# A gated mix of long convolution and attention on one core: five probability tiles instead of four, one copy instead of two of two small tiles

## The chip, the core and the metric

The kernel runs on one core of a Trainium2 chip. The time is device microseconds (us) of one execution; the number that counts is the median of several executions. The engines are TensorE (PE in the profile, its weight loads PEld), VectorE (DVE), ScalarE (ACT), GpSimd (POOL) and SyncE (SP), whose queue issues most of the DMAs.

## What is computed

For x of 2048 tokens by 640, the result is `g * a + (1 - g) * b`, with a gate g per token. Cut to what matters:

```python
g = sigmoid((x * gate_w).sum(-1, keepdims=True))
# a: a shifted product kv = (4-tap shift of k) * v, convolved with a 2048-tap filter per channel
kv = k_shift * v
y = irfft(rfft(kv, 4096) * rfft(ssm_k, 4096))[:2048] + kv * ssm_D
a = q * y                                  # q is x
# b: attention of 32 heads of width 20 over one shared k and v
scores = einsum("bhqd,bkd->bhqk", x @ wq, x @ wk) * 20 ** -0.5
b = einsum("bhqk,bkd->bhqd", softmax(scores), x @ wv) @ wo
out = g * a + (1 - g) * b
```

## The kernel before, in words

The attention is cut into 512 rounds (u = 0 to 511): four blocks of 512 queries (index I), eight groups of four heads (g) in each, sixteen chunks of 128 keys (j) in each group. A round has, for four heads, 128 keys and 512 queries:

- QK (L897 to L912): four matmuls of 21 rows each that work side by side in the array and write four PSUM banks, that is two pairs of banks. There are three such pairs (banks 0 to 5), used in turn.
- EXP (L914 to L922): two instructions of ScalarE, h = 0 and h = 1, each over one pair of banks (128x1024), which write bf16 probabilities to one of the tiles ET0 to ET3. The slot is `(2 * u + h) % 4`. In rounds j = 2 and j = 9 of most groups VectorE computes h = 1 instead, in five instructions (DEXP, L924 to L940), into the tile ETd.
- PV (L948 to L968): four matmuls of 32 columns each, side by side, that add probabilities times v into bank 6. After sixteen rounds VectorE copies bank 6 out (`acc`, L1002), and a chain of small DMAs and VectorE instructions divides by the sum and stores the group (`norm`, L998 to L1015).

The program's order of the attention on PE is fixed: after EXP(u, 0) come QK(u+1), EXP(u, 1) and PV(u-1) (L976 to L993). The rest of the kernel, the convolution as cosine and sine matmuls (L1098 to L1214, spectra, product on GpSimd, inverse), query projections (`qproj`, L832) and the output projection (`oproj`, L1217), is put between these by a list scheduler (L133 to L370). It runs a clock of its own with assumed costs and places, on each engine, what is ready: on PE the next attention matmul if it is ready, else a group of other matmuls that fits in the gap (L237 to L303). Where its own account of PE is under half busy in the last 2.4 us and a gap is left, it places a matmul over a tile of zeros that is there only to keep PE working (L290 to L294, emitted from L1278). The order that comes out is then static; at run time each engine works through its list in order and waits on semaphores, one for each dependence on another engine's instruction, a tile's earlier reader among them.

Two small tiles belong to the change as well. `cr` (two copies, L602) holds a row that VectorE writes (L862) and a DMA takes into the query tile (L865). `ytmp` (two copies, L617) holds the sum that VectorE makes of an inverse group (L1208) and that the next VectorE instruction multiplies (L1212).

The output projection has eight groups of five matmuls per block I. The groups of blocks 0 to 2 may use bank 7 alone (L1230), so that each waits for VectorE's copy of the one before (L1235).

Of the kernel before, what the change touches and what calls it, by code (L numbers as in the profile page):

```python
# [479 lines left out]
class Kernel:  # L480

    def __init__(self, nc, aps):
        self.nc = nc
        self.aps = aps
        self.g = Graph()
        self.T = {}
        self.nb = 0
        self.late_pv = []


# [47 lines left out]
    def alloc(self):  # L538
# [30 lines left out]
        sb("Tsin0", [128, NF, 128], BF16)  # L569
        sb("Tsinv0", [128, 1024], BF16)  # L570
        sb("zeros", [128, 128], BF16)
        for i in range(4):
            sb(f"ET{i}", [128, 1024], BF16)
        sb("ETd", [128, 1024], BF16)
        sb("dJ", [128, 1024], dt.uint32)
# [23 lines left out]
        for i in range(4):  # L599
            sb(f"sq{i}", [128, 512], BF16)  # L600
        sb("ci", [16, 512], I32)
        for i in range(2):  # L602
            sb(f"cr{i}", [16, 512], BF16)
        sb("acc", [128, 512], F32)
        sb("den", [128, 16], F32)
        sb("rcp", [128, 16], F32)
# [7 lines left out]
                 ("vslab0", [128, D], BF16), ("vslab1", [128, D], BF16), ("vslab2", [128, D], BF16),  # L614
                 ("kprod", [128, 4, D], BF16), ("kshs", [128, 2, D], BF16), ("w4", [128, 4, D], BF16)]
        late = [("AB0", [128, NF, 2, 2, CW], BF16), ("AB1", [128, NF, 2, 2, CW], BF16),
                ("ytmp0", [128, 512], BF16), ("ytmp1", [128, 512], BF16)]  # L617
        spec = []
        for i in range(3):
            spec += [(f"X{i}", [128, 2, 2, CW], BF16), (f"K{i}", [128, 2, 3, CW], BF16)]  # L620
# [211 lines left out]
    def qproj(self, I, gs, prio, banks, ng):  # L832

        T = self.T
        qt = T[f"qT{I % 2}"]
        par = I % 2
        for gl, gi in enumerate(gs):
            gr = self.group("qp", prio, banks=banks)
            for dc in range(NDC):
                self.mm(gr, lambda e, bk, gi=gi, dc=dc: e.matmul(  # L840
                    self.bank(bk), T["wq_pad"][:, dc, 128 * gi:128 * gi + 128],
                    T["xT"][:, dc, 512 * I:512 * I + 512], start=(dc == 0), stop=(dc == NDC - 1)),
                    [("wq_pad", 0 if gi < 2 else 1), ("xT", I)], c_mm(512))
            self.evac(gr, "dve", None, (), [("qT", par, gi)], 0.7,
                      alts=self.copy_alts(qt[:, gi, :], lambda bk: self.bank(bk)))
            self.dve(lambda e, gi=gi, gl=gl: e.tensor_tensor(T[f"sq{gl}"][:, :], qt[:, gi, :], qt[:, gi, :],
                                                             ALU.mult),
                     [("qT", par, gi)], [("sq", gl)], c_fast(512), prio=prio - 500, port=True, name="sq")
        gr = self.group("q2", prio - 500, banks=banks)
        ind = T[f"IndG{ng}"]  # L850
        for gl in range(ng):
            self.mm(gr, lambda e, bk, gl=gl: e.matmul(self.bank(bk)[0:4 * ng, :], ind[:, gl, :], T[f"sq{gl}"][:, :],
                                                      start=(gl == 0), stop=(gl == ng - 1)),
                    [f"IndG{ng}", ("sq", gl)], c_mm(512))
        n = 4 * ng
        self.nb += 1
        ck = self.nb % 2
        ci, cr = T["ci"], T[f"cr{ck}"]
        self.evac(gr, "dve", lambda e, bk: e.tensor_scalar(
            ci[0:n, :], self.bank(bk)[0:n, :].bitcast(I32), 0.5, float(0x1FBD1DF5), ALU.mult, ALU.add), (),  # L860
            ["ci"], c_ps(512))
        self.dve(lambda e: e.tensor_scalar(cr[0:n, :], ci[0:n, :].bitcast(F32), T["kmaxr"][0:n, 0:1], -UP,  # L862
                                           ALU.mult, ALU.add), ["ci", "kmaxr"], [("cr", ck)], c_fast(512), prio=prio - 500,
                 name="root")
        o = self.dma(qt[20:128:32, gs[0]:gs[0] + ng, :], cr[0:n, :], reads=[("cr", ck)],  # L865
                 writes=[("qT", par, gi) for gi in gs], nbytes=n * 1024, prio=prio - 500, name="crow")
        if I == 0 and gs[0] == 0:
            self.crow0 = [o]
# [20 lines left out]
    def attention(self, I):  # L889
# [23 lines left out]

        def EXP(u, h):  # L914
            p = pairs(u)[h]
            slot = (2 * u + h) % 4
            if h == 1 and on_dve(u):
                return DEXP(u, p)
            op("act", lambda e, p=p, slot=slot: e.activation(  # L919
                T[f"ET{slot}"][:, :], self.ps[:, 1024 * p:1024 * p + 1024], ACT.Exp, scale=SCALE),  # L920
                [("ps", 2 * p), ("ps", 2 * p + 1)], [("ET", slot)], 0.91, name="exp", main=True,
                after=self.sins if u == 0 else ())  # L922
# [25 lines left out]
        def PV(u):  # L948
            j = u % 16
            rs = (0, 1) if on_dve(u) else (0, 1, 2, 3)  # L950
            for r in rs:
                slot = (2 * u + r // 2) % 4
                o = PVmm(r, j, T[f"ET{slot}"], ("ET", slot), cost=0.03 if r < rs[-1] else 0.27, main=True,
                         cont=(r > 0), banks=(6,))
                o.last = j == NSC - 1
# [225 lines left out]
    def inverse(self, c, q, prio):  # L1181
        T = self.T
        AB = T[f"AB{c % 2}"]
        n = 4 * c + q
        yt = T[f"ytmp{n % 2}"]
        gr = self.group("inv", prio)
        for h in range(2):
            ci = 2 * q + h
# [12 lines left out]
        def toks(t):  # L1201
# [5 lines left out]
        rk = [("kvc", c, 0), ("kvc", c, 1), ("kvc", c, 2), ("kvc", c, 3)]  # L1207
        self.evac(gr, "dve", lambda e, bk: e.tensor_tensor(  # L1208
            y4, self.bank(bk).rearrange("p (i b c) -> p i b c", i=2, b=2), kvp, ALU.add), rk,
            [("ytmp", n % 2)], c_ps(512))  # L1210
        ids = [2 * q, 2 * q + 1, NF + 2 * q, NF + 2 * q + 1]
        self.dve(lambda e: e.tensor_tensor(kvp, y4, xg, ALU.mult),  # L1212
                 [("ytmp", n % 2)] + [("xg", i) for i in ids], [("A", i) for i in ids],
                 c_fast(512), prio=prio - 1000, port=True, name="amul", after=())  # L1214


# [116 lines left out]
```

## Time and profile before

| what | value |
| --- | --- |
| runs | 1022.82, 1033.32, 1030.26 us; median 1030.26 |
| the profiled execution | 1036.53 us, span 1034.7 us |
| mean TensorE clock in it | 0.95 |
| first EXP starts, last EXP starts | 43.4, 984.9 us |
| busy in the span: PE, DVE, ACT, POOL | 837.3, 641.0, 936.3, 384.0 us |

The span runs from the first to the last instruction; the time holds 1.8 us more. All durations come from this one execution, which lies 6.3 us above the median of the three runs. The busy time of ScalarE is a union of its instructions, and consecutive ones overlap a little, so that a short wait of one can hide as less overlap; a gap is named as a wait only from 150 ns up.

### The profile page before, as it was taken

The page shows a single profiled execution, that of the slowest core. Times are in us where ns is not written, and L with a number is a line of the kernel's source. Part 1 is how long each engine was busy: PE and PEld are TensorE (multiplying, and loading weights), DVE is VectorE, ACT ScalarE, POOL GpSimd, SP SyncE. Part 2 cuts the span into 40 slices and gives each one's busy share as a digit, 9 for nine tenths or more (in the row PEclk, how much of TensorE's full clock was granted, in tenths as well). Part 3 has the DMA queues.
Part 4 walks back from the last instruction along what each step waited for, and adds up shares of the span by engine and source line. Part 5 has one row for each costly group of instructions (what it writes and reads, how often), then busy time and mean ns, then how long its engine had stood idle before and what let it go on. Part 6 is the DMA issues. An engine that isn't in the chain of part 4 may idle for free.

```text
span 1034.7 us, 16679 instructions
## 1 busy us (share of the span) xinstructions
PE 837.3 (81%) x6874; PEld 348.6 (34%) x6949; DVE 641.0 (62%) x954; ACT 936.3 (90%) x1007; POOL 384.0 (37%) x427
## 2 busy tenths in 40 slices
PE   6677777888888888888888888887888988888865
PEld 4122113433334333344333333442234433323322
DVE  8577972336675677655676666665775566644632
ACT  6499999998899999999999999998999999998910
POOL 2360000784154336651316541434652546620000
PEclk9799999998899999999999999998899999998985
DMA  5312731001000000000000100000000000012221
GB/s 149 122 33 91 237 104 54 11 12 37 16 17 17 12 18 27 17 16 17 16 18 16 37 18 12 15 9 16 16 17 17 17 16 12 12 54 57 67 76 42
DMA packets 34626, 40.57 MB, mean 39 GB/s; under 512 B 12796, under 2 KB 27766, under 8 KB 34550
## 3 DMA queue, kind: packets, MB, share of 16 engines
q1 hardware_dynamic: 32582, 39.25, 12.1%
q8 instruction: 54, 0.88, 0.4%
q10 hardware_dynamic: 1968, 0.26, 0.2%
q14 instruction: 22, 0.18, 0.1%
HBM read 32.03 MB, written 7.08 MB: 38 GB/s over the span
## 4 chain that ended last, share of the span: by engine, by line
ACT 69%; PE 22%; DMA 5%; DVE 3%; issue 1%; SPq 0%; ACTq 0%
ACT ET L919 68%; PE ps L903 5%; PE ps L943 5%; PE ps L1122 4%; PE ps L1197 3%; PE ps L1232 2%; DMA rbc<-scr_d 2%; PE ps L840 1%; DVE outsb L1235 1%; PE ps L1278 1%; DMA qT<-cr 1%; DMA scr_d<-rcp 1%; PE ps L784 0%; DMA xn<-in_A_q_dram 0%; DMA wo<-in_B_wo_dram 0%
## 5 line engine op out<-in xcount | busy, mean ns | idle before, releaser
L919 ACT ACTIVATE ET<-ps 128x1024 bf16<-128x1024 f32 x972 | 912.7, 1021 | 35.9 <-PE ps L943 26.5
L1160 POOL TENSOR_TENSOR Pp<-X,K 128x256 f32<-128x256 bf16 x240 | 198.7, 854 | 404.6 <-DVE K L1150 272.4
L903 PE MATMUL ps<-qT,kT 21*128 21x512 bf16 x2048 | 227.7, 395 | 146.5 <-ACT ET L919 137.9
L943 PE MATMUL ps<-ET,vaug 128*32 128x512 bf16 x1944 | 210.8, 398 | 0.4 <-ACT ET L919 0.4
L903 PEld LDWEIGHTS ps<-qT,kT 21*128 21x128 bf16 x2048 | 56.6, 91 | 316.8 <-ACT ET L919 304.9
L1160 POOL TENSOR_TENSOR V<-Pp 128x256 f32<-128x256 f32 x80 | 70.7, 884 | 69.9 <-DVE AB L1177 67.1
L943 PEld LDWEIGHTS ps<-ET,vaug 128*32 128x32 bf16 x1944 | 52.6, 93 | 118.9 <-issue 115.3
L931 DVE TENSOR_SCALAR dJ<-ps 128x1024 uint32<-128x1024 f32 x52 | 63.6, 1224 | 45.9 <-PE ps L903 45.5
L1278 PE MATMUL ps<-Tcos,zeros 128*128 128x512 bf16 x252 | 80.6, 401 | 6.2 <-issue 6.2
L1197 PE MATMUL ps<-AB,Tcos 128*128 128x256 bf16 x320 | 77.3, 278 | 2.3 <-DVE ytmp L1208 2.0
L938 DVE SCALAR_TENSOR_TENSOR dJ<-dJ 128x1024 f32<-128x1024 uint16 x52 | 70.4, 1353 | 0.4
L936 DVE SCALAR_TENSOR_TENSOR dE<-dJ,dE 128x1024 f32<-128x1024 uint16 x52 | 69.0, 1328 | 0.5
L939 DVE SCALAR_TENSOR_TENSOR ETd<-dJ,dE 128x1024 bf16<-128x1024 f32 x52 | 69.2, 1330 | 0.2
L1197 PE MATMUL ps<-AB,Tsin 128*128 128x256 bf16 x280 | 68.5, 278 | 0.0
L1160 POOL TENSOR_TENSOR Pp<-Pp 128x512 f32<-128x512 f32 x40 | 59.9, 1498 | 2.8
L1002 DVE COPY acc<-ps 128x512 f32<-128x512 f32 x32 | 22.1, 691 | 61.7 <-PE ps L943 61.6
L1139 DVE TENSOR_SCALAR K<-ps 128x256 bf16<-128x256 f32 x35 | 14.8, 423 | 58.8 <-PE ps L1122 58.7
L1012 DVE TENSOR_TENSOR oTn<-acc,rbc 128x512 bf16<-128x512 f32 x32 | 27.6, 862 | 37.3 <-DMA rbc<-scr_d 37.2
L1232 PE MATMUL ps<-wo,oTp 128*128 128x320 bf16 x160 | 36.5, 370 | 17.2 <-DVE outsb L1235 13.7
L1122 PE MATMUL ps<-kv,Tsin 128*128 128x256 bf16 x320 | 49.8, 279 | 0.0
L1122 PE MATMUL ps<-ssm_kT,Tsin 128*128 128x256 bf16 x320 | 49.7, 281 | 0.0
L1122 PE MATMUL ps<-ssm_kT,Tcos 128*128 128x256 bf16 x320 | 47.7, 282 | 2.3 <-DVE X L1134 1.2
(127 smaller groups left out, 847.4 us busy)
## 6 DMA issues: line engine op xcount, KB each, us to landing
kslab<-in_A_k_dram SPq DMA_DIRECT2D x15, 640.0 KB
rbc<-scr_d SPq DMA_DIRECT2D x32, 256.0 KB
scr_o<-oTn SPq DMA_DIRECT2D x32, 128.0 KB
xn<-in_A_q_dram SPq DMA_DIRECT2D x4, 640.0 KB
vslab<-in_A_v_dram SPq DMA_DIRECT2D x16, 160.0 KB, 4.2
kst<-in_A_ssm_k_dram SPq DMA_DIRECT2D x5, 512.0 KB
oTp<-scr_o SPq DMA_DIRECT2D x16, 160.0 KB, 2.9
out_dram<-outsb SPq DMA_DIRECT2D x16, 160.0 KB
```

The costliest lines, as they stand in the source:

```text
L903: o = op("pe", lambda e, r=r, Iu=Iu, g=g, j=j, bk=banks[r]: e.matmul(self.bank(bk), T["kT4"][32 * r:32 * r + 21, 128 * j:128 * j + 128], T ...
L919: op("act", lambda e, p=p, slot=slot: e.activation(T[f"ET{slot}"][:, :], self.ps[:, 1024 * p:1024 * p + 1024], ACT.Exp, scale=SCALE), [("p ...
L931: V(lambda e, p=p: e.tensor_scalar(J[:, :], self.ps[:, 1024 * p:1024 * p + 1024], SCALE * LOG2E * 65536.0, EOFF * 65536.0, ALU.mult, ALU.add),
L936: V(lambda e: e.scalar_tensor_tensor(Ef, lo, ED, Ef, ALU.add, ALU.mult), ["dJ", "dE"], ["dE"], c_ps(1024), **k)
L938: V(lambda e: e.scalar_tensor_tensor(Jf, lo, EP, lo, ALU.add, ALU.mult), ["dJ"], ["dJ"], c_ps(1024), **k)
L939: V(lambda e: e.scalar_tensor_tensor(T["ETd"][:, :], Jf, EQ, Ef, ALU.add, ALU.mult), ["dJ", "dE"], ["ETd"], c_ps(1024), **k)
L943: return op("pe", lambda e, r=r, j=j, src=src: e.matmul(self.bank(6)[32 * r:32 * r + 32, :], T["vaug"][:, j, :], src[:, 512 * (r % 2):512 ...
L1122: o = self.mm(gr, lambda e, bk, lhs=lhs, rhs=rhs, comp=comp, n=n: e.matmul(self.bank(bk, 256, 256 * comp), lhs, rhs, start=(n == 0), stop= ...
L1160: self.pool(lambda e: e.tensor_tensor(out, a, b, alu), reads, writes, c_pool(n), prio=prio, port=True, name="mac")
L1197: self.mm(gr, lambda e, bk, lhs=lhs, fc=fc, comp=comp, h=h: e.matmul(self.bank(bk, 256, 256 * h), lhs, AB[:, fc, :, comp, :], start=(fc == ...
L1232: self.mm(gr, lambda e, bk, kc=kc, ci=ci, n0=n0: e.matmul(self.bank(bk, HD), op[:, kc, 128 * ci:128 * ci + 128], T["wo"][:, kc, n0:n0 + HD ...
L1278: sch.filler = lambda e: e.matmul(self.bank(6), self.T["zeros"][:, :], self.T["Tcos"][:, 0, 0:512], start=False, stop=False)
```

## The change

A fifth probability tile is added, and the slot of a round's half becomes `(2 * u + h) % 5`. `cr` and `ytmp` have one copy each instead of two.

```diff
-        self.nb = 0
@@ alloc
-        for i in range(4):
+        for i in range(5):
             sb(f"ET{i}", [128, 1024], BF16)
...
-        for i in range(2):
-            sb(f"cr{i}", [16, 512], BF16)
+        sb("cr", [16, 512], BF16)
...
-                ("ytmp0", [128, 512], BF16), ("ytmp1", [128, 512], BF16)]
+                ("ytmp", [128, 512], BF16)]
@@ qproj
-        ci, cr = T["ci"], T[f"cr{ck}"]
+        ci, cr = T["ci"], T["cr"]
...
-                                           ALU.mult, ALU.add), ["ci", "kmaxr"], [("cr", ck)], c_fast(512), prio=prio - 500,
+                                           ALU.mult, ALU.add), ["ci", "kmaxr"], ["cr"], c_fast(512), prio=prio - 500,
...
-        o = self.dma(qt[20:128:32, gs[0]:gs[0] + ng, :], cr[0:n, :], reads=[("cr", ck)],
+        o = self.dma(qt[20:128:32, gs[0]:gs[0] + ng, :], cr[0:n, :], reads=["cr"],
@@ EXP
-            slot = (2 * u + h) % 4
+            slot = (2 * u + h) % 5
@@ PV
-                slot = (2 * u + r // 2) % 4
+                slot = (2 * u + r // 2) % 5
@@ inverse
-        yt = T[f"ytmp{n % 2}"]
+        yt = T["ytmp"]
...
-            [("ytmp", n % 2)], c_ps(512))
+            ["ytmp"], c_ps(512))
...
-                 [("ytmp", n % 2)] + [("xg", i) for i in ids], [("A", i) for i in ids],
+                 ["ytmp"] + [("xg", i) for i in ids], [("A", i) for i in ids],
```

Since the scheduler sees other dependences, its whole order comes out anew: the same matmuls, but 298 instead of 319 over the tile of zeros. Two places on PE follow. Lines of the changed program are 4 or 5 lower (L899 is L903 of before, L939 is L943, L1118 is L1122, L1192 is L1197, L1227 is L1232, L1273 is L1278).

Rounds 204 to 206 on PE, before (qT: QK; ET: PV; zeros: the matmuls over zeros):

```order
L903 MATMUL ps<-qT1,kT4 128x512 x4
L943 MATMUL ps<-ET0,vaug 32x512 x2
L943 MATMUL ps<-ET1,vaug 32x512 x2
L1278 MATMUL ps<-Tcos,zeros 128x512 x2
L903 MATMUL ps<-qT1,kT4 128x512 x4
L943 MATMUL ps<-ET2,vaug 32x512 x2
L943 MATMUL ps<-ET3,vaug 32x512 x2
L1278 MATMUL ps<-Tcos,zeros 128x512 x2
```

The same rounds now:

```order
L899 MATMUL ps<-qT1,kT4 128x512 x4
L939 MATMUL ps<-ET4,vaug 32x512 x2
L939 MATMUL ps<-ET0,vaug 32x512 x2
L1273 MATMUL ps<-Tcos,zeros 128x512 x3
L899 MATMUL ps<-qT1,kT4 128x512 x4
L939 MATMUL ps<-ET1,vaug 32x512 x2
L939 MATMUL ps<-ET2,vaug 32x512 x2
L1118 MATMUL ps<-ssm_kT1_78,Tcos 128x256 x8
```

QK still stands ahead of the PV of two rounds earlier; the tiles go round in fives; a convolution group stands where two matmuls over zeros stood, one round earlier than before.

The end of PE's list, before, from the last QK on (oTp: the output projection):

```order
L903 MATMUL ps<-qT1,kT4 128x512 x4
L943 MATMUL ps<-ET2,vaug 32x512 x2
L943 MATMUL ps<-ET3,vaug 32x512 x2
L943 MATMUL ps<-ET0,vaug 32x512 x2
L943 MATMUL ps<-ET1,vaug 32x512 x2
L1232 MATMUL ps<-wo_84,oTp1_86 128x320 x5
L943 MATMUL ps<-ET2,vaug 32x512 x2
L943 MATMUL ps<-ET3,vaug 32x512 x2
L1232 MATMUL ps<-wo_84,oTp1_86 128x320 x30
L1232 MATMUL ps<-wo_84,oTp0_85 128x320 x40
L1232 MATMUL ps<-wo_84,oTp1_86 128x320 x40
```

And now, right behind the last PV (AB: the inverse of the convolution):

```order
L1192 MATMUL ps<-AB0_80,Tsin 128x256
L1192 MATMUL ps<-AB0_80,Tcos 128x256
L1192 MATMUL ps<-AB0_80,Tsin 128x256
L1192 MATMUL ps<-AB0_80,Tcos 128x256
L1192 MATMUL ps<-AB0_80,Tsin 128x256
L1192 MATMUL ps<-AB0_80,Tcos 128x256
L1192 MATMUL ps<-AB0_80,Tsin 128x256
L1192 MATMUL ps<-AB0_80,Tcos 128x256
L1192 MATMUL ps<-AB0_80,Tsin 128x256
L1227 MATMUL ps<-wo_83,oTp1_85 128x320 x40
L1227 MATMUL ps<-wo_83,oTp0_84 128x320 x40
L1227 MATMUL ps<-wo_83,oTp1_85 128x320 x40
```

Nine matmuls of an inverse group and 24 groups of the output projection now stand behind the last PV, where 22 groups stood behind it before.

The end of SP's queue, before, from the last group's store on (oTp1: loads of the last block's projection input, one for each quarter; outsb: stores of output rows, which wait for the projection):

```order
L501 DMA scr_o<-oTn 128x512
L501 DMA out_0_dram<-outsb0_87 128x640
L501 DMA oTp1_86<-scr_o 32x5x512
L501 DMA out_0_dram<-outsb1_88 128x640
L501 DMA oTp1_86<-scr_o 32x5x512
L501 DMA out_0_dram<-outsb2_89 128x640
L501 DMA oTp1_86<-scr_o 32x5x512
L501 DMA out_0_dram<-outsb3_90 128x640
L501 DMA oTp1_86<-scr_o 32x5x512
```

And now:

```order
L500 DMA scr_o<-oTn 128x512
L500 DMA out_0_dram<-outsb2_88 128x640
L500 DMA oTp1_85<-scr_o 32x5x512
L500 DMA out_0_dram<-outsb3_89 128x640
L500 DMA oTp1_85<-scr_o 32x5x512
L500 DMA out_0_dram<-outsb0_86 128x640
L500 DMA oTp1_85<-scr_o 32x5x512
L500 DMA out_0_dram<-outsb1_87 128x640
L500 DMA oTp1_85<-scr_o 32x5x512
```

The last load stood behind all four stores of block 2 (outsb0 to outsb3); now it stands behind the first two of them.

3 lines of the change are left out of this document (removed).

## The prediction

> **What bounds the kernel now.** I read the page first, then the waits of ScalarE, its exponentials (line L919) by stretches, the timeline of one full-clock round, the clock by stretches, and last the tail.
>
> ```profile
> PE 837.3 (81%) x6874; PEld 348.6 (34%) x6949; DVE 641.0 (62%) x954; ACT 936.3 (90%) x1007; POOL 384.0 (37%) x427
> L919 ACT ACTIVATE ET<-ps x972: 1018/1023/1045, 43.4 to 984.9; 128x1024 bf16<-128x1024 f32 x195
> ACT ET L919 <- PE ps L943: 26.5, 27, 2.7
> ACT ET L919 <- PE ps L903: 6.1, 1, 6.1
> ```
>
> ScalarE is the busiest engine, and 972 exponentials run from 43.4 to 986 us. The waits say who stops them: 27 waits, 26.5 us, ended by PV (L943), and none by QK (L903) but the first of all. An exponential does not read what PV writes. It waits for PV because PV is the last reader of the ET tile that it is going to overwrite. That is a wait for a buffer.
>
> The waits of the list begin at 150 ns. Shorter ones show in single starts:
>
> ```profile
> 399.96 1.02 ACT L919 ACTIVATE ET<-ps 128x1024 bf16<-128x1024 f32 x1
> 400.91 1.02 ACT L919 ACTIVATE ET<-ps 128x1024 bf16<-128x1024 f32 x1
> 401.83 1.02 ACT L919 ACTIVATE ET<-ps 128x1024 bf16<-128x1024 f32 x1
> 402.77 1.02 ACT L919 ACTIVATE ET<-ps 128x1024 bf16<-128x1024 f32 x1
> 400.12 0.39 PE L903 MATMUL ps<-qT,kT 21*128 21x512 bf16 x4 [0.38 <-ACT ET L919]
> 400.44 0.40 PE L943 MATMUL ps<-ET,vaug 128*32 128x512 bf16 x4
> 401.98 0.39 PE L903 MATMUL ps<-qT,kT 21*128 21x512 bf16 x4 [0.60 <-ACT ET L919]
> 402.31 0.40 PE L943 MATMUL ps<-ET,vaug 128*32 128x512 bf16 x4
> ```
>
> The starts alternate by 0.95, 0.92, 0.94 us. Second halves (at 401.83) come 0.92 after the first; first halves (400.91, 402.77) come 0.02 to 0.03 later than that. The loop closes through PE: an exponential ends at 400.98 - 0.92 = 400.06, QK starts at 400.12, PV at 400.44, PV ends at 400.84, and the exponential after next starts at 400.91. QK of the same round is done at 400.51, 0.33 us earlier. So with four tiles a round at full clock takes 1.86 us where two exponentials back to back take 1.84, and anything that makes PE late shows at once.
>
> ```profile
> 43.40:283.00 239.60, 188.92 (x1490) 69.39 (x1509) 144.65 (x242) 228.67 (x245) 82.64 (x103) 0.93 0.22 71
> 283.00:552.00 269.00, 230.20 (x2002) 99.88 (x2022) 180.85 (x253) 266.72 (x285) 120.29 (x133) 1.00 0.06 17
> 552.00:986.00 434.00, 365.05 (x3060) 153.29 (x3094) 270.42 (x350) 417.35 (x444) 174.56 (x177) 0.96 0.08 24
> 986.00:1034.70 48.70, 27.69 (x112) 11.29 (x112) 13.57 (x25) 0.00 (x0) 0.00 (x0) 0.64 0.19 63
> ACT ET L919 <- PE ps L943: 1.8, 3, 0.7
> ```
>
> These are stretches of the run: length, busy time and count of PE, PEld, DVE, ACT and POOL, then the granted clock; the last line gives the PV waits of 283 to 552 alone. From 43.4 to 986 us are 942.6 us; 972 exponentials at 0.92 would be 894. So 48 us are lost: 26.5 in named waits, 21.5 in waits too short to be named. In the stretch at full clock the named ones are 1.8 us for 285 exponentials; over 972 that rate makes 6. The other 20 lie in or beside stretches of half clock, which make 0.07 x 2 x 239.6 + 0.04 x 2 x 434 = 68 us.
>
> ```profile
> 224.90:228.30 3.40, 3.13 (x32) 1.71 (x28) 1.10 (x3) 3.40 (x5) 2.85 (x4) 1.00 0.02 5
> 228.30:231.70 3.40, 2.01 (x23) 0.62 (x20) 2.14 (x3) 3.40 (x4) 3.24 (x5) 1.00 0.02 2
> 231.70:235.10 3.40, 3.40 (x19) 1.05 (x16) 2.74 (x5) 2.15 (x3) 0.86 (x2) 0.50 0.03 2
> 235.10:238.50 3.40, 3.40 (x19) 1.62 (x19) 0.92 (x2) 2.04 (x3) 0.00 (x0) 0.50 0.19 69
> ```
>
> After a stretch with PE busy 2.01 of 3.40 us the clock is half for two stretches; PE is then busy all the time, and ScalarE loses 1.25 and 1.36 us.
>
> **The change part by part.** *The fifth tile, short waits.* EXP(u+1, 0) is number 2u+2 and overwrites the tile of number 2u-3, whose PV stands before QK(u+1) on PE; before it was number 2u-2, whose PV stands behind it. So a first half now waits for QK alone, which ends 0.33 us before PV did. A lateness under 0.15 us disappears in that. The bound above is all 21.5 us, the bound below none (a rival). I take 18: QK itself is late where a group of other matmuls runs over, and in half clock. What is late next is QK: it can be 0.33 us late before it costs anything.
>
> *The fifth tile, named waits.* At full clock, 6 us in some 10 waits, each shorter by up to 0.33: 3 us. At half clock the lead of QK over PV is larger:
>
> ```profile
> 707.26 0.61 PE L903 MATMUL ps<-qT,kT 21*128 21x512 bf16 x4
> 707.81 0.62 PE L943 MATMUL ps<-ET,vaug 128*32 128x512 bf16 x4
> 708.49 1.02 ACT L919 ACTIVATE ET<-ps 128x1024 bf16<-128x1024 f32 x1 [2.15 <-PE ps L943]
> ```
>
> It is 0.55 us. But there PE has more work than time (3.40 busy of 3.40), so a tile more lets ScalarE run ahead once, not in every round. Above: 17 waits by 0.55, 9 us; below: 0. I take 1. Together 4 us, between 0 and 12.
>
> The Trainium skill (TensorE: Matmul & The Clock Gate, "HAM oscillation — how this bites in real kernels") lets the clock fall to half after an idle gap of about 3.4 us. The rows differ: it fell behind a stretch in which PE was busy for 2.01 us, so a thin stretch is enough here. By the page's rule no half clock would arise between two exponentials at all, the term at half clock would be 0 instead of 1, and the rival on the clock below would fall away.
>
> *The front.* `cr` with one copy makes the second row (L862) wait until the first DMA out of it has landed:
>
> ```profile
> 35.14 0.69 SPq L501 DMA_DIRECT2D qT<-cr  x1
> 39.41 0.47 DVE L862 TENSOR_SCALAR cr<-ci,kmaxr 8x512 bf16<-8x512 f32 x1
> 42.69 0.61 PE L903 MATMUL ps<-qT,kT 21*128 21x512 bf16 x4 [4.78 <-DMA qT<-cr]
> 46.91 0.69 DVE L534 CAST qT<-ps 128x512 bf16<-128x512 f32 x1 [6.62 <-PE ps L840]
> 44.49 9.10 SPq L501 DMA_DIRECT2D qT<-cr  x2
> 52.57 0.47 DVE L862 TENSOR_SCALAR cr<-ci,kmaxr 8x512 bf16<-8x512 f32 x1
> ```
>
> QK starts at 42.69 on that landing, so L862 moves from 39.41 to about 42.7 and holds VectorE for 3.3 us. Behind it stand one copy of 0.47 and the evacuation at 46.91, before which VectorE is idle for 6.62 us: cost 0 through this cover, 3.3 us without it. The third row is written at 52.57, 8.1 us after the second DMA went out at 44.49; the first took 7.5 to 42.69, so this one waits little or not at all. `ytmp` adds waits of VectorE for itself, in order anyway: 0.
>
> *The tail.* The order puts nine matmuls of an inverse group and 24 instead of 22 projection groups behind the last PV.
>
> ```profile
> 980.62 0.69 DVE L1208 TENSOR_TENSOR ytmp<-ps,kv 128x512 bf16<-128x512 f32 x1 [1.79 <-PE ps L1197]
> 986.28 0.85 PE L1232 MATMUL ps<-wo,oTp 128*128 128x320 bf16 x5
> 987.78 0.85 PE L1232 MATMUL ps<-wo,oTp 128*128 128x320 bf16 x5 [0.65 <-DVE outsb L1235]
> 989.28 0.85 PE L1232 MATMUL ps<-wo,oTp 128*128 128x320 bf16 x5 [0.65 <-DVE outsb L1235]
> 1004.93 1.51 PE L1232 MATMUL ps<-wo,oTp 128*128 128x320 bf16 x5 [0.65 <-DVE outsb L1235]
> 1007.09 1.51 PE L1232 MATMUL ps<-wo,oTp 128*128 128x320 bf16 x5 [0.65 <-DVE outsb L1235]
> 1014.29 1.51 PE L1232 MATMUL ps<-wo,oTp 128*128 128x320 bf16 x5 [3.53 <-DMA oTp<-scr_o]
> 978.22 0.28 PE L1197 MATMUL ps<-AB,Tsin 128*128 128x256 bf16 x1
> 978.34 0.27 PE L1197 MATMUL ps<-AB,Tcos 128*128 128x256 bf16 x1
> ```
>
> A group takes 1.50 us at full clock and 2.16 at half, bound by PE and VectorE in turn. Two more: +4.3 at half clock. The inverse ahead of them (nine matmuls 0.11 apart, the last's end 0.2 later, VectorE 0.69 in the same bank): +2. The last load of oTp was issued behind all four stores of block 2 and PE waited 3.53 us for it; it now stands behind two, with four groups of cover: -3. The sum is +3.5, between 0 (full clock for longer) and +7 (half clock from the start).
>
> *Sum* against the profiled execution: 1036.5 - 18 - 4 + 3.5 = 1018. The median of the runs is 1030.3, 6 us lower; it holds less half clock, where part of the gain lies, so I take 16 instead of 18.5 from it: **1014 us**.
>
> **The rivals.** *The 0.02 us is ScalarE's own.* If a first half costs more because it waits on PE at all, it keeps its 0.94. Then 21.5 shrinks to the waits of 0.05 us and more: some 460 first halves at 0.023 are 10.6 us that stay, and the gain is 16 - 10 = 6: 1024. For it: the offset is nearly constant. Against: PV's end at 400.84 and the start at 400.91 agree with a wait that PV ends.
>
> *The clock, slower than before.* The place is the thin rounds, in which PE has QK, PV and matmuls over zeros alone; 298 of these are left of 319. Price: ScalarE loses 1.3 us in each 3.4 us stretch at half clock, of which 68 / 3.4 = 20 were there. It decides from 12 more on (16 us, the whole gain); with twenty more, 1014 + 26 = 1040. For it: the order leaves out 21 such matmuls, and 2.01 of 3.40 was not enough. Against: rounds are shorter too, so PE is thinner in fewer us; rounds 204 to 206 carry as much work as before. By the Trainium skill's page this rival has no place; by the rows it has.
>
> *The gain ends in the tail.* The exponentials end earlier, but the projection's loads and groups don't keep up, at the upper bound of the tail and with the front's 3.3: 1014 + 3.5 + 3.3 = 1021. For it: work moved behind the last PV already. Against: the tail's loads are earlier in SP's queue.
>
> **How the numbers follow.** The forecast has 0.68, the first rival 0.14, the clock 0.10, the tail 0.08. A measurement of this kernel tells about 1% from no change: under 1020.0 is faster, over 1040.6 slower. The forecast's own range is 1003 (21.5 and 9 us gained, tail 3) to 1022; up to 1030 it takes in the rivals but the clock. Faster: 0.68 less a twentieth for its own upper end, 0.65. Slower: half of the clock rival and a little for what I don't see, 0.07. Within 1%: the rest, 0.28.
>
> **What would show it.** Right: waits of L919 for L943 near zero, and what is left of its waits ended by L903; a full-clock stretch with starts 0.92 apart throughout; the last exponential at about 963 to 968 us instead of 985, in an execution with as much half clock; a tail of some 52 us. Wrong: first halves still at 0.94 (first rival); a granted clock under 0.93 before the last exponential (second); a tail over 55 us (third).

## The result, and the profile after

| kernel | runs, us | median | ratio to before |
| --- | --- | --- | --- |
| before | 1022.82, 1024.26, 1030.26, 1033.32 | 1027.26 | 1 |
| changed | 988.32, 991.41, 995.67, 1006.67 | 993.54 | 0.9651, 95% interval 0.9567 to 0.9735 |

The ratio compares fast runs alone and so leaves out the run of 1006.67 us; the profiled execution of before, 1036.53 us, is a slow one too, which is why a second pair of profiles, both of fast runs, stands beside the first below. The change makes the kernel 3.5% faster. The forecast was 1014 us with a range from 1003 to 1030: the direction was right, the gain is twice what was forecast (33.7 us between the medians against 16), and the result lies under the range. The profiled execution took 995.67 us, its span 993.9. Of its page, the busy time of TensorE and the rest, and the group of the exponentials (L915 is L919 of before):

```profile
PE 820.1 (83%) x6862; PEld 342.9 (35%) x6928; DVE 640.4 (64%) x954; ACT 917.5 (92%) x1007; POOL 379.4 (38%) x427
L915 ACT ACTIVATE ET<-ps 128x1024 bf16<-128x1024 f32 x972 | 893.9, 1181 | 20.5 <-PE ps L899 20.4
```

The same line by itself (durations in ns: least, median, most; first and last start), and then in the list of waits (total, times, longest):

```profile
L915 ACT ACTIVATE ET<-ps x972: 1017/1186/1323, 43.7 to 950.7; 128x1024 bf16<-128x1024 f32 x195
```

```profile
ACT ET L915 <- PE ps L899: 20.4, 19, 6.2
```

The waits for PV are gone: none of 150 ns or more is left of 27. What remains is ended by QK (L899), 19 waits, of which the longest, 6.2 us, is the one ahead of the first exponential and stood in before as well. The last exponential starts at 950.7 instead of 984.9.

One number looks wrong: the same instruction, 1.02 us long in before, now lasts 1.19 us in the median, and yet all of them are done 34 us earlier. Four in a row at full clock show how (start and duration):

```profile
404.30 1.16 ACT L915 ACTIVATE ET<-ps 128x1024 bf16<-128x1024 f32 x1
405.20 1.18 ACT L915 ACTIVATE ET<-ps 128x1024 bf16<-128x1024 f32 x1
406.11 1.19 ACT L915 ACTIVATE ET<-ps 128x1024 bf16<-128x1024 f32 x1
407.01 1.20 ACT L915 ACTIVATE ET<-ps 128x1024 bf16<-128x1024 f32 x1
```

The starts are 0.90 apart, but start and duration added give ends at 405.46, 406.38, 407.30 and 408.21, which are (408.21 - 405.46) / 3 = 0.917 apart. A start that waits for nothing is recorded a little earlier each time, and the record grows by about 0.012 us per instruction, up to 1.32 us. So the pace of ScalarE is read from the ends: 0.917 us, which is also the median over all 971 distances between ends. 972 x 0.917 = 891.3 us is the least that the exponentials can take.

The stretch of the exponentials and the tail, of the changed kernel (length, busy time and count of PE, PEld, DVE, ACT, POOL, then the granted clock, DMA share and GB/s):

```profile
43.70:952.00 908.30, 773.06 (x6520) 317.71 (x6583) 593.24 (x840) 893.93 (x973) 373.00 (x412) 0.97 0.11 35
952.00:993.90 41.90, 21.95 (x131) 10.66 (x131) 15.81 (x29) 0.00 (x0) 0.00 (x0) 0.98 0.23 77
```

Front, exponentials and tail add up to the span, so the difference of the two profiled executions is told by them. The exponentials are split once more: what each distance between two ends has over 0.917 us is counted over the whole trace, and put to half clock where it lies in a stretch that the clock's records show at half, or in the microsecond behind one. A second profiled execution of each kernel (the last two experiments) stands beside the first.

| us | before | after | difference | second execution of each |
| --- | --- | --- | --- | --- |
| front, to the first exponential | 43.4 | 43.7 | +0.3 | 42.1, 43.8: +1.7 |
| exponentials | 942.5 | 908.2 | -34.3 | 942.9, 907.5: -35.4 |
| of it lost at full clock | 23.9 | 2.2 | -21.7 | 25.0, 2.2: -22.8 |
| of it lost at half clock | 27.2 | 14.6 | -12.6 | 26.5, 13.8: -12.7 |
| tail | 48.8 | 41.9 | -6.9 | 45.6, 43.5: -2.1 |
| time at half clock in the exponentials | 62.1 | 47.3 | | 69.2, 47.3 |
| time at half clock in the tail | 35.0 | 1.7 | | 21.7, 6.0 |

What is left at half clock looks like this in the changed kernel (the columns as above):

```profile
237.80:241.20 3.40, 2.31 (x28) 1.03 (x26) 2.33 (x4) 3.40 (x5) 3.08 (x5) 1.00 0.02 5
241.20:244.60 3.40, 3.40 (x22) 1.56 (x18) 2.55 (x4) 2.59 (x3) 0.00 (x0) 0.50 0.55 154
244.60:248.00 3.40, 2.62 (x27) 1.02 (x24) 2.00 (x2) 3.06 (x4) 1.96 (x2) 1.00 0.00 0
```

As in before, the clock falls behind a thin stretch (PE busy for 2.31 of 3.40 us). In the stretch at half clock PE has no time left over, and ScalarE idles for 0.81 us in it and 0.34 in the one behind it, 1.15 in all.

### The profile page after: what moved, and what is told of

It is laid out like the page before. It is cut to its first block, busy times and chain, and to the rows that moved or that the text cites. A ratio compares the mean times of both kernels' runs of the same rounds, so it can differ in the third digit from the quotient of the medians.

```text
span 993.9 us, 16644 instructions
## 1 busy us (share of the span) xinstructions
PE 820.1 (83%) x6862; PEld 342.9 (35%) x6928; DVE 640.4 (64%) x954; ACT 917.5 (92%) x1007; POOL 379.4 (38%) x427
## 3 DMA queue, kind: packets, MB, share of 16 engines
q1 hardware_dynamic: 32582, 39.25, 12.7%
## 4 chain that ended last, share of the span: by engine, by line
ACT 81%; PE 11%; DVE 4%; DMA 3%; issue 1%; ACTq 0%; SPq 0%; DVEq 0%
ACT ET L915 81%; PE ps L899 2%; PE ps L1227 2%; DMA rbc<-scr_d 1%; PE ps L1192 1%; PE ps L838 1%; PE ps L939 1%; DVE outsb L1230 1%; PE ps L1118 1%; DMA qT<-cr 1%; DVE tprod L709 0%; PE ps L782 0%; DVE dJ L927 0%; PE ps L769 0%; PE ps L1273 0%
## 5 line engine op out<-in xcount | busy, mean ns | idle before, releaser
L915 ACT ACTIVATE ET<-ps 128x1024 bf16<-128x1024 f32 x972 | 893.9, 1181 | 20.5 <-PE ps L899 20.4
L1156 POOL TENSOR_TENSOR Pp<-X,K 128x256 f32<-128x256 bf16 x240 | 192.8, 830 | 398.3 <-DVE K L1146 261.0
L899 PE MATMUL ps<-qT,kT 21*128 21x512 bf16 x2048 | 225.8, 392 | 124.8 <-ACT ET L915 113.1
L939 PE MATMUL ps<-ET,vaug 128*32 128x512 bf16 x1944 | 209.4, 395 | 0.4 <-ACT ET L915 0.4
L899 PEld LDWEIGHTS ps<-qT,kT 21*128 21x128 bf16 x2048 | 56.2, 91 | 294.7 <-ACT ET L915 276.0
L1156 POOL TENSOR_TENSOR V<-Pp 128x256 f32<-128x256 f32 x80 | 72.8, 910 | 60.5 <-DVE AB L1173 57.7
L939 PEld LDWEIGHTS ps<-ET,vaug 128*32 128x32 bf16 x1944 | 52.4, 93 | 118.7 <-issue 113.9
L927 DVE TENSOR_SCALAR dJ<-ps 128x1024 uint32<-128x1024 f32 x52 | 63.6, 1224 | 36.8 <-PE ps L899 36.6
L1273 PE MATMUL ps<-Tcos,zeros 128*128 128x512 bf16 x241 | 75.8, 390 | 6.5 <-issue 6.4
L1192 PE MATMUL ps<-AB,Tcos 128*128 128x256 bf16 x320 | 77.2, 277 | 0.6 <-DVE K L1137 0.6
L932 DVE SCALAR_TENSOR_TENSOR dE<-dJ,dE 128x1024 f32<-128x1024 uint16 x52 | 71.8, 1380 | 0.5
L1192 PE MATMUL ps<-AB,Tsin 128*128 128x256 bf16 x280 | 67.8, 275 | 0.0
L1128 DVE CAST X<-ps 128x256 bf16<-128x256 f32 x40 | 16.9, 422 | 58.3 <-PE ps L1118 58.3
L838 PE MATMUL ps<-xT,wq_pad 128*128 128x512 bf16 x151 | 46.5, 424 | 6.4 <-DVE qT L533 2.5
L1118 PE MATMUL ps<-kv,Tcos 128*128 128x256 bf16 x320 | 49.4, 289 | 1.7 <-DVE K L1137 0.9
L1118 PE MATMUL ps<-kv,Tsin 128*128 128x256 bf16 x320 | 48.8, 279 | 0.0
L1008 DVE TENSOR_TENSOR oTn<-acc,rbc 128x512 bf16<-128x512 f32 x32 | 24.0, 750 | 38.5 <-DMA rbc<-scr_d 38.3
L1118 PE MATMUL ps<-ssm_kT,Tsin 128*128 128x256 bf16 x320 | 48.7, 274 | 0.0
```

The source lines that it names most:

```text
L838: self.mm(gr, lambda e, bk, gi=gi, dc=dc: e.matmul(self.bank(bk), T["wq_pad"][:, dc, 128 * gi:128 * gi + 128], T["xT"][:, dc, 512 * I:512 ...
L899: o = op("pe", lambda e, r=r, Iu=Iu, g=g, j=j, bk=banks[r]: e.matmul(self.bank(bk), T["kT4"][32 * r:32 * r + 21, 128 * j:128 * j + 128], T ...
L915: op("act", lambda e, p=p, slot=slot: e.activation(T[f"ET{slot}"][:, :], self.ps[:, 1024 * p:1024 * p + 1024], ACT.Exp, scale=SCALE), [("p ...
L927: V(lambda e, p=p: e.tensor_scalar(J[:, :], self.ps[:, 1024 * p:1024 * p + 1024], SCALE * LOG2E * 65536.0, EOFF * 65536.0, ALU.mult, ALU.add),
L932: V(lambda e: e.scalar_tensor_tensor(Ef, lo, ED, Ef, ALU.add, ALU.mult), ["dJ", "dE"], ["dE"], c_ps(1024), **k)
L939: return op("pe", lambda e, r=r, j=j, src=src: e.matmul(self.bank(6)[32 * r:32 * r + 32, :], T["vaug"][:, j, :], src[:, 512 * (r % 2):512 ...
```

## The experiments

In the first three, the order of every engine's instructions is planned with one set of tiles and then used, instruction by instruction, with another. This parts the change in two: what the order brings, and what the tiles bring at run time. In the diffs a pair holds the number of probability tiles and whether `cr` and `ytmp` have two copies. The expectations were written while the start-to-start distance was still taken for ScalarE's pace; where they speak of 0.92 or 0.904 apart, starts are meant.

**The order of before, the tiles of the change.**

```diff
+ORDER_OF, TILES_OF = (4, True), (5, False)
...
+        first = self.plan(*ORDER_OF)
+        first.run()
+        order = {e: [(None if o.name == "fill" else o.seq, None if o.grp is None else o.grp.bank)
+                     for o in first.order[e]] for e in ENGS}
+        sch = self.plan(*TILES_OF)
+        sch.forced(order)
```

> The order of every engine is that of the kernel before, kept word for word; only the tiles are those of the change (five ET, one cr, one ytmp). Theory A, the tile itself pays at run time: waits of the exponentials for PV gone, starts 0.91 to 0.92 us apart, the stretch of exponentials 905 to 920 us instead of 942.5, the tail as before at 42 to 49 us, the whole at 995 to 1008 us. Theory B, the new order of the scheduler pays: within 1% of before, 1020 to 1035 us, first halves still 0.94 apart.

Measured: 999.35 us against 1030.32, ratio 0.9689 (0.9624 to 0.9754). Its waits (the exponentials are L977, QK L961, PV L1001 here and in the next three kernels):

```profile
ACT ET L977 <- PE ps L961: 20.1, 20, 6.2
```

The fifth tile at run time, in an order that was made for four, has the gain: the interval holds the change's own ratio. No wait for PV is left. Half clock in the exponentials falls from 62 to 34 us in the same order.

**The order of the change, four tiles.** One copy of the small tiles.

```diff
-ORDER_OF, TILES_OF = (4, True), (5, False)
+ORDER_OF, TILES_OF = (5, False), (4, False)
```

> The order of every engine is that of the changed kernel; the tiles at run time are four ET (one cr, one ytmp). Theory A: waits for PV are back, the stretch of exponentials is 935 to 945 us, 1020 to 1035 us in all (less if the tail stays at full clock, 42 us). Theory B: 990 to 1000 us as with the change.

**The order of before, four tiles, one copy of the small tiles.**

```diff
-ORDER_OF, TILES_OF = (4, True), (5, False)
+ORDER_OF, TILES_OF = (4, True), (4, False)
```

> The order of before and four ET tiles, but one cr and one ytmp: the small tiles alone. Theory A and theory B: within 1% of before, 1020 to 1035 us; VectorE holds its second cr row until the first has landed at about 42.7 us and nothing else moves. A rival, that the small tiles cost something which the fifth tile hides: 3 us or more slower.

Measured: 1029.49 us, ratio 0.997 (0.9925 to 1.0014) for the new order; 1029.51 us, 0.9978 (0.9948 to 1.0009) for the small tiles. The waits of the exponentials with the new order, and then with the order of before:

```profile
ACT ET L977 <- PE ps L1001: 17.2, 27, 1.6
ACT ET L977 <- PE ps L961: 6.2, 1, 6.2
```

```profile
ACT ET L977 <- PE ps L1001: 28.8, 30, 2.9
ACT ET L977 <- PE ps L961: 6.4, 1, 6.4
```

Neither the new order nor the small tiles changes the time by what can be measured. With four tiles PV ends the waits in both orders, and both lose the same at full clock, 24.3 and 23.1 us. The new order has shorter waits (17 against 29 us) and half clock in 51 instead of 68 us, which its median doesn't show: its profiled execution took 1023.15 us, 6 us less than its median.

**No matmuls over zeros.** The change, with the threshold under which the planner places them set to nothing.

```diff
-FILL = 0.5
+FILL = 0.0
```

> The change without the matmuls over zeros (the share under which the scheduler places them set from 0.5 to 0). If thin stretches of PE bring the half clock and it costs ScalarE 1.3 us in each 3.4 us, the granted clock before the last exponential falls well under 0.9, with 60 stretches or more at half clock and 1030 us or more in all, against 994 for the change. If the half clock is not tied to how thin PE's work is: 990 to 1005 us.

Measured: 1039.52 us, ratio 1.0097 (1.0059 to 1.0136). The exponentials' stretch and their waits:

```profile
43.40:990.00 946.60, 779.54 (x6297) 310.49 (x6309) 593.91 (x845) 899.61 (x973) 376.90 (x412) 0.86 0.11 34
```

```profile
ACT ET L915 <- PE ps L899: 52.3, 57, 6.0
```

Without the zeros the fifth tile's whole gain is gone and a little more. The clock is half for 263.5 us (77 times 3.4) in 31 pieces instead of 47.3 us in 9; 52.4 us are lost there, and at full clock 2.7 us as with the zeros. So the clock could have taken the gain back, as the second rival said; with 298 matmuls over zeros left it did not.

**More matmuls over zeros.**

```diff
-FILL = 0.5
+FILL = 0.6
```

> The change with more matmuls over zeros (placed where PE's planned share is under 0.6 instead of 0.5; 431 instead of 298). If thin stretches bring the half clock, fewer of them: under 25 us of half clock between the first and the last exponential instead of 47, and 983 to 993 us. If the added matmuls make QK late instead: more waits for QK at full clock, 995 us or more.

Measured: 992.43 us, ratio 0.9629 (0.9586 to 0.9672), which can't be told from the change. With 431 of them the exponentials have 23.2 us at half clock and lose 8.6 us there instead of 14.6, but the tail of this profiled execution is 46.5 us long, 15.5 of them at half clock.

**Four tiles, PV ahead of QK.** If what is paid is the wait for the PV that stands behind QK, four tiles must do where PV(u-1) stands ahead of all four matmuls of QK(u+1). The two are swapped in PE's list of before.

```diff
...
+            if what[k:n] == ["qk"] * 4:
+                m = n
+                while m < len(what) and what[m] == "pv" and first.g.all[order["pe"][m][0]].main:
+                    m += 1
+                swapped += order["pe"][n:m] + order["pe"][k:n]
...
```

> Four ET tiles, one cr and one ytmp, and the order of before with one thing moved: wherever a whole QK stands right ahead of a PV on PE, the PV is put ahead of the QK (rounds whose QK is split in two keep their order). Then the PV that a first half waits for is over before QK begins, with four tiles. Theory A, the wait for PV was the cost, however it is taken away, and without it ScalarE's own pace is 0.904 us and not 0.92: starts 0.904 apart in most rounds, the stretch of exponentials 908 to 925 us, 995 to 1012 us in all. Rival C, the fifth tile pays by something else than this wait (its address, or more room between ScalarE's writes and PE's reads): first halves still at 0.94, 1020 us or more. Rival D: a PV that waits for VectorE's copy of bank 6 now holds QK behind it, and the gain is lost there: waits of the exponentials for QK over 40 us.

Measured: 1015.55 us against 1029.45, ratio 0.9861 (0.9832 to 0.989). The exponentials and what they wait for:

```profile
L977 ACT ACTIVATE ET<-ps x972: 1018/1072/1323, 41.8 to 967.9; 128x1024 bf16<-128x1024 f32 x195
```

```profile
ACT ET L977 <- PE ps L961: 26.6, 22, 5.9
ACT ET L977 <- PE ps L1001: 3.5, 6, 1.3
```

The time is over the 995 to 1012 us of theory A, and under the 1020 of rival C. Without a fifth tile the starts at full clock are now 0.904 apart in the median for first and second halves alike, and the loss at full clock falls from 24 to 12.3 us. So the 0.02 us of first halves were a wait for PV and nothing of ScalarE's own. The rest stays: QK is now late instead, above all in the two rounds behind one in which VectorE has the second half. There, at full clock, the first halves end 7.3 us later, taken together, than at 0.917 us each (2.6 us in the first of the two rounds, 4.7 in the second). At half clock it loses 23.4 us, little less than the order of before. The tile frees both, the swap only one.

**A sixth tile.** `ytmp` and the tile of zeros move into a tile that is free after the projection of the keys, which makes room for one more.

```diff
...
-        for i in range(5):
+        for i in range(6):
             sb(f"ET{i}", [128, 1024], BF16)
...
-            slot = (2 * u + h) % 5
+            slot = (2 * u + h) % 6
...
-        yt = T["ytmp"]
+        yt = T["wk4"][:, :, :].rearrange("p a b -> p (a b)")[:, 0:512]
...
```

> The change with six ET tiles; ytmp and the tile of zeros lie in a tile that is no longer used by then. Theory A: with five tiles no exponential waits for a tile any more, what is left are waits for QK, so a sixth brings nothing: within 1% of the change, 985 to 1004 us. Rival: more room lets ScalarE run ahead through stretches at half clock: 980 us or less.

Measured: 986.5 us, ratio 0.9582 (0.9511 to 0.9652). The exponentials' waits:

```profile
ACT ET L914 <- PE ps L898: 12.4, 9, 7.1
```

At full clock nothing more is won, 3.0 us lost against 2.2. At half clock it loses 3.7 us in 16.3 us. By itself the median is not clearly under the change's, since the intervals overlap.

**The attention's banks for the output projection.** The change, with banks 0 to 6 released to the projection's groups once the last PV is placed.

```diff
+        if m is None and any(self.bank_claimed.values()):
+            for x in range(7):
+                ends = [self.g.writer[("ps", x)]] + self.g.readers[("ps", x)]
+                if self.bank_claimed[x] and all(o.placed for o in ends):
+                    self.bank_claimed[x] = False
+                    self.bank_last[x] = ends
...
-                gr = self.group("op", pr + ci, banks=(7,) if I < 3 else (7, 6, 5, 4, 3, 2, 1, 0))
+                gr = self.group("op", pr + ci, banks=(7, 6, 5, 4, 3, 2, 1, 0))
```

> The change with one thing more: when the last PV is placed, the scheduler gives the attention's seven banks to the projection groups, so that in the tail PE need not wait for VectorE's copy of the group before. The stretch of exponentials as with the change, 905 to 915 us. The tail: 24 groups at 0.67 to 0.75 instead of 1.5 us, until the chain of the last group's DMAs is the bound: 26 to 32 us instead of 41.9, 978 to 988 us in all. If the tail was bound by that chain already: 40 us or more.

Measured: 986.1 us, ratio 0.9589 (0.9534 to 0.9645); tail 37.0 us. TensorE and the loads of the last block in the tail:

```profile
957.13 11.03 PE L1234 MATMUL ps<-wo,oTp 128*128 128x320 bf16 x80
970.69 8.08 SPq L507 DMA_DIRECT2D oTp<-scr_o  x4
980.81 8.12 PE L1234 MATMUL ps<-wo,oTp 128*128 128x320 bf16 x40 [12.65 <-DMA oTp<-scr_o]
```

The ping-pong with VectorE is gone: 16 groups take 11.03 us instead of 16 x 1.50 = 24. But then PE stands for 12.65 us, because the last group's sums and stores are done only at 970.69, and the four loads behind them take until 980.8. Most of what the banks save is lost to that new wait, and the tail is over the 26 to 32 us expected. The profiled execution, 994.55 us, is the longest of the four, and the interval overlaps the change's, so that this median alone doesn't show a saving either.

**Six tiles and the free banks**, the edits of the last two together.

> Six probability tiles, and the attention's banks given to the output projection once the last PV is placed: the two edits that each came out near 986 us against 993.5 of the change. Theory (both save on their own: the sixth tile by fewer waits for QK and fewer half-clock stretches in the exponentials, the banks in the tail): 979 to 983 us, a ratio to before of about 0.953; exponentials from first start to last end 898 to 905 us, starts 0.904 apart; tail 33 to 38 us. Rival (what looked like two savings is the scatter of half clock between executions): 985 to 994 us, the ratio within 0.003 of the change's own in this job. Where the last part of the tail still waits for the load of the last block's projection input, the tail stays at 35 or more whatever the banks do.

**The same with more zeros.**

```diff
-FILL = 0.5
+FILL = 0.6
```

> The kernel of the run before with the threshold for matmuls over zeros at 0.6 instead of 0.5. Theory (six tiles leave few half-clock stretches, 16 us in the profiled execution, so more zeros have little left to save): within 3 us of the kernel of the run before, clock 0.98 or more. Rival (the zeros still pay): 5 us or more faster than it. If more zeros delay QK, waits for QK rise over 16 us and it is slower.

Measured, in one job with the change: 979.61 us, ratio 0.9495 (0.9451 to 0.954); with more zeros 985.51 us, 0.9557 (0.9508 to 0.9606); the change itself 997.03 us, 0.9678 (0.9618 to 0.9739). Stretch of the exponentials and tail of the first:

```profile
40.60:939.80 899.20, 774.00 (x6595) 317.54 (x6595) 608.57 (x850) 892.78 (x973) 386.04 (x412) 0.99 0.12 36
939.80:976.30 36.50, 18.02 (x117) 11.84 (x117) 14.10 (x26) 0.01 (x1) 0.00 (x0) 0.80 0.25 84
```

And the waits of the exponentials with more zeros:

```profile
ACT ET L921 <- PE ps L905: 18.2, 14, 7.1
```

Together the two beat the change by 1.7%, with intervals apart: 979.61 / 997.03 = 0.983. The exponentials take 899.2 us, 8 more than ScalarE needs, with 16.7 us at half clock. It came out as the theory had it, and the scatter falls as an explanation. More zeros don't help here: the median is 5.9 us higher, with intervals that overlap, waits for QK are 18.2 us against 13.5, and half clock is 26.6 us in the profiled execution. That is the last of the three cases in its expectation, as far as it can be told from no change.

**Both kernels once more**, unchanged, each for a second profile.

> The kernel before, unchanged, for a second profiled execution. Theory (the order does not fix the clock; half clock in the exponentials and in the tail differs from one execution to the next, the spacing at full clock does not): first halves again 0.944 apart and second halves 0.920; half clock in the exponentials anywhere from 50 to 75 us; a tail of about 42 us if it runs at full clock and up to 49 us if it falls to half. Rival (the tail of 48.8 us and the 62.1 us at half clock belong to the order): both come again within 1.5 us and 4 us.

> The changed kernel, unchanged, for a second profiled execution. Theory: ratio to before 0.962 to 0.970; starts again 0.904 apart for both halves; half clock in the exponentials 25 to 50 us, under all that of the kernels with four tiles in the usual order (51 to 68 us); the tail 40 to 47 us by whether it runs at full clock. Rival (half clock in the exponentials is scatter and has nothing to do with the tiles): it comes out over 51 us in the profiled execution.

Measured: 1031.13 us, ratio 1.0 (0.9962 to 1.0037), and 997.03 us, 0.9678. Exponentials and tail of before, and then of the change:

```profile
42.10:985.00 942.90, 802.74 (x6622) 322.16 (x6621) 596.21 (x842) 913.57 (x973) 377.01 (x412) 0.96 0.11 34
985.00:1030.70 45.70, 24.46 (x112) 10.44 (x112) 13.57 (x25) 0.04 (x1) 0.00 (x0) 0.76 0.21 67
```

```profile
43.80:951.30 907.50, 785.31 (x6583) 317.62 (x6582) 592.79 (x840) 894.06 (x973) 372.35 (x412) 0.97 0.11 35
951.30:994.80 43.50, 23.23 (x131) 11.00 (x131) 15.79 (x29) 0.00 (x0) 0.00 (x0) 0.93 0.22 74
```

The exponentials come out the same to 1 us, and most of the changed kernel's half clock lies at the same places (near 112, 241, 255, 286, 550, 577 and 900 us). So what happens there belongs for the most part to the order and the tiles. That the total is 47.3 us both times is luck: the first execution has 10.2 us near 354 that the second lacks, and the second has stretches near 705 and 883; before has 62.1 and 69.2 us. The tail does scatter: 48.8 and 45.6 us before, 41.9 and 43.5 after.

The profiles of all of these kernels, with losses and half clock counted as above:

| kernel | tiles, order | lost at full clock | at half clock: time, lost | tail (of it half clock) |
| --- | --- | --- | --- | --- |
| before, twice | 4, before | 23.9, 25.0 | 62.1, 27.2; 69.2, 26.5 | 48.8 (35.0), 45.6 (21.7) |
| small tiles alone | 4, before | 23.1 | 67.9, 30.1 | 42.6 (8.0) |
| new order alone | 4, changed | 24.3 | 51.0, 17.1 | 44.8 (8.5) |
| PV ahead of QK | 4, swapped | 12.3 | 61.4, 23.4 | 45.6 (20.5) |
| tiles alone | 5, before | 5.1 | 33.8, 12.2 | 45.3 (19.1) |
| the change, twice | 5, changed | 2.2, 2.2 | 47.3, 14.6; 47.3, 13.8 | 41.9 (1.7), 43.5 (6.0) |
| no zeros | 5, own | 2.7 | 263.5, 52.4 | 43.8 (20.2) |
| more zeros | 5, own | 3.6 | 23.2, 8.6 | 46.5 (15.5) |
| free banks | 5, own | 5.3 | 51.4, 15.3 | 37.0 (13.7) |
| six | 6, own | 3.0 | 16.3, 3.7 | 38.8 (2.4) |
| six, free banks | 6, own | 3.3 | 16.7, 4.5 | 36.5 (14.4) |
| the same, more zeros | 6, own | 3.0 | 26.6, 10.4 | 36.8 (14.0) |

## Why the prediction was right or wrong, step by step

*What bounds the kernel, and the short waits: right.* The prediction took 18 us for waits too short to be named and 3 for named ones at full clock, 21 together. Measured at full clock: 23.9 - 2.2 = 21.7 us, and 22.8 in the second pair. It holds by parts too, in the first pair: 19.6 us behind waits under 150 ns and 2.0 behind named ones. The fifth tile at run time brings it, in either order; the new order with four tiles and the small tiles bring nothing. The base was slightly off: 0.92 us is the distance of starts behind a wait, ScalarE's pace is 0.917, so the loss in before was 51 us and not 48. The 68 us at half clock came from rounded clock means; the clock's records have 62.1.

*Named waits at half clock: the step that failed.* "There PE has more work than time, so a tile more lets ScalarE run ahead once, not in every round. Above: 17 waits by 0.55, 9 us; below: 0. I take 1." Measured: 12.6 and 12.7 us, over the step's upper bound too. Two terms are in it. Before lost 27.2 us in 62.1 us of half clock, that is 1.49 for each 3.4 us, and the change 14.6 in 47.3, 1.05 for each 3.4 us.

- Each stretch costs less: 47.3 / 3.4 x (1.49 - 1.05) = 6.1 us. Run ahead once by 0.55 us in each of the 11 stretches of before makes 11 x 0.55 = 6.0; the step's 1 counted the run-ahead once in the program and not once in each stretch. The agreement is in part luck, since the new order has a share in the 6.1: with the order held, 3.4 us at half clock cost 1.30 to 1.51 with four tiles and 1.23 with five (order of before), 1.14 and then 1.05 and 0.99 (order of the change). At eleven places, stretches at half clock of the same length stand at the same rounds in executions of one order with four and with five tiles; with five they lose 0.37 us less on the mean, from 0.61 less (rounds 0 to 3 in the order of before) to 0.19 more (rounds 490 to 492). So the run-ahead in each stretch is there, and it is worth some 4 us of the 12.6.
- There is less half clock: (62.1 - 47.3) / 3.4 x 1.49 = 6.5 us. The prediction held the time at half clock fixed, but for a rival in which it grew. In the second pair these two are 4.3 and 8.4 us.

That a tile more cuts the time at half clock is shown for the order of before, 62.1, 69.2 and 67.9 us with four tiles and 33.8 with five; for the new order the difference is small, 51.0 against 47.3. Why a stretch falls away isn't shown. It may be that PE, when the exponentials no longer wait for it, has its idle time spread over more rounds and has fewer thin stretches, but no run isolates that.

*What makes the clock fall: the row held, but it is no rule.* The prediction set its row (half clock behind a stretch with PE busy 2.01 of 3.40 us) above the Trainium skill's TensorE: Matmul & The Clock Gate, "HAM oscillation — how this bites in real kernels", by whose gap of about 3.4 us no half clock would arise in the exponentials. The traces since agree with the row: 2.31 of 3.40, and 31 pieces at half clock without the zeros; and PE never stands idle for 3.4 us between the first and the last exponential, 2.03 us at most in before and 1.40 in the change. But a thin stretch does not bring the fall each time: in before PE is busy for 2.12 of 3.41 us from 241.94 us on and the clock stays full behind it, while it falls at 552.6 behind 2.66 of 3.41. The next section of that page, "A second HAM failure mode: psum-queue depth-cycling", does speak of many short idle times between groups of matmuls as a cause, and this kernel is of that kind; the prediction should have weighed that one.

*The front: right.* SP sends the first row of `cr` out, VectorE writes the second (L858 is L862 of before), and then evacuates:

```profile
35.40 0.69 SPq L500 DMA_DIRECT2D qT<-cr  x1
43.09 0.98 DVE L858 TENSOR_SCALAR cr<-ci,kmaxr 8x512 bf16<-8x512 f32 x1 [3.37 <-DMA qT<-cr]
47.26 0.69 DVE L533 CAST qT<-ps 128x512 bf16<-128x512 f32 x1 [2.79 <-PE ps L838]
```

VectorE is held for 3.37 us (forecast 3.3), and the cover is there: it still waits 2.79 us for PE before the evacuation. The first exponential starts 0.3 us later, and 1.7 in the second pair; the other kernels with four or five tiles start theirs between 41.8 and 43.8, so that this can't be told from scatter.

*The tail: wrong in sign.* Forecast +3.5 us, measured -6.9 and -2.1. The stall of the last load went as foreseen. The waits of the tail's matmuls in the changed kernel, and in the second execution of before:

```profile
PE ps L1227 <- DVE outsb L1230: 15.3, 23, 1.1
PE ps L1227 <- DVE ytmp L1203: 0.8, 1, 0.8
```

```profile
PE ps L1232 <- DVE outsb L1235: 13.6, 20, 1.4
PE ps L1232 <- DMA oTp<-scr_o: 3.7, 1, 3.7
```

The term that failed is the clock of the tail. The forecast has "Two more: +4.3 at half clock" and leaves the groups of before at half clock as they were; the tail of the changed kernel runs almost wholly at full clock, all 24 groups at 1.50 us. A group at half clock takes 2.16, 0.66 more, so 35.0 us at half clock less the stall of 3.53 cost (35.0 - 3.5) / 2.16 x 0.66 = 9.6 us in before. By the prediction's other numbers the tail would be 48.8 - 9.6 - 3.5 + 3.0 for two groups + 2 for the inverse = 40.7; it is 41.9. So a tail at full clock is 8 us shorter, where the forecast had 0 as its bound for "full clock for longer". (Its three terms, 4.3 + 2 - 3, also add to 3.3 and not 3.5.) In the second pair the same working gives (21.7 - 3.7) / 2.16 x 0.66 = 5.5 us for half clock and 45.6 - 5.5 - 3.7 + 3.0 + 2 = 41.4 at full clock; it is 43.5 with 6.0 us at half. Whether the order keeps the clock up isn't settled: the order of before had 35.0, 21.7, 19.1 and 8.0 us at half clock in four executions, the new one 1.7, 6.0 and 8.5 in three. In either order a tail of 42 to 45 us occurs, so that the sign of the difference isn't settled either.

*The sum and the step to the median.* Forecast against the profiled execution: -18 - 4 + 3.5 = -18.5. Measured: -21.7 - 12.6 + 0.3 - 6.9 = -40.9 (1036.53 to 995.67), and in the second pair -22.8 - 12.7 + 1.7 - 2.1 = -35.9. The medians differ by 33.7 us. Of the 22 us missing in the forecast, 12 are half clock in the exponentials and 10 the tail, again for the most part the clock. The range had its lower end from the bounds 21.5 and 9 us gained and a tail of +3; both bounds on what the clock does were passed. Its other bounds, 12 us for all named waits and 0 for the tail, were not used for the range; with them it would have begun at 1036.5 - 21.5 - 12 - 6.3 = 997, still over 993.5.

*The rivals.* The first (0.02 us is ScalarE's own) fell: with no wait, first and second halves start 0.904 apart and end 0.917 apart, with four tiles too once PV is ahead of QK. The second (more half clock) didn't happen, though the kernel without zeros shows its mechanism. The third (the gain ends in the tail) fell with the tail at 42 to 43.5 us.

*What would show it.* The waits came as written: none for PV, the rest for QK. The starts, 0.90 apart rather than 0.92, and the last exponential at 950.7 rather than 963 to 968 were the signs of the larger gain.

## What to carry to other kernels

Where the busiest engine waits for a buffer's last reader, and that reader stands behind a producer it also waits for, one buffer more can pay for every short wait as well as for the named ones, as here, and a run with the old order and the new buffer tells in one step which of the two brings the gain. Before costing such a change, take the engine's own pace from the ends of instructions that wait for nothing, and count the named waits by the state of the clock: a run-ahead that helps once in each half-clock stretch is worth up to its length times the number of stretches (here 0.37 of 0.55 us in each on the mean). Time at half clock is not a constant of the kernel; it needs a term with two bounds and two signs.

## What the runs showed of the hardware that was not expected

- ScalarE's records overlap when it waits for nothing: an exponential over 128x1024 lasts 1.02 us behind a wait and up to 1.32 us in a row of unhindered ones, with starts 0.904 and ends 0.917 apart. The mean duration of the group rose from 1021 to 1181 ns while its union of busy time fell from 912.7 to 893.9 us.
- The clock fell to half behind stretches of 3.4 us with PE busy for 2.01 and 2.31 us of them, though PE was never idle for more than 2.03 us between the first and the last exponential of these two executions; behind another stretch with 2.12 us busy it did not fall. The places recur for the most part from one execution to the next in the exponentials. In the tail, where PE and VectorE take turns on one bank, it stayed at half for 8 to 35 us in four executions of one order.
- Without matmuls over zeros, 263.5 of 946.6 us of exponentials ran at half clock; 298 such matmuls leave 47.3 us, at a difference of 46 us in the median (1039.52 against 993.54).
